# Five token blocks instead of six in two chained feed-forward networks, with rotating tiles for the halves of x

## The chip, the cores and the metric

The kernel runs on one core of a Trainium2 chip. The metric is the device time of one execution in microseconds (us). Before the change the median of three runs is 928.14 us (928.04 to 928.32).

## The reference

A window attention over 4 batches, 8 heads, 512 local and 32 global positions and head size 64 makes 2176 tokens of width 512. They pass through two feed-forward networks, one after the other, each with its own weights (512 x 2048 and 2048 x 512, given as float64):

```python
x = attention(q_l, k_l, v_l, q_g, k_g, v_g)   # 2176 x 512
h = x @ w_in;  x = (h * cos(h)) @ w_out       # network 0
h = x @ w2_in; out = (max(h, 0) ** 2) @ w2_out  # network 1
```

## The kernel before, in words

Every matrix is held as a high half and a low half in a reduced float32 format, and a product is three matmuls: high by high, low by high, high by low. The attention fills `xt`, the tokens by columns: 4 chunks (`kk`) of 128 features, 2176 columns. Then come the networks, which are one list of steps (`steps`). A step takes one block of token columns and one of the 16 chunks of 128 hidden units of its network (`g` 0 to 15 and 16 to 31). The chunks come in groups, 4, 5 and 7 in network 0 and 8 and 8 in network 1. Within a group the loop runs over the blocks, and within a block over the chunks of the group. So chunks 9 to 15 are first used in the first block of network 0's third group. With six blocks there are 96 steps in each network.

`ffn_step(s)` writes one step's instructions in a fixed order. On TensorE (PE) they are `g1` of step s (12 matmuls into `h`, one for each `kk` and each of the three products, as wide as the block), then `g2` of step s-3 into `y`. In network 0 `g2` is 12 matmuls as wide as the block; in network 1 the roles are turned, and it is three matmuls of width 512 for every 128 tokens of the block. ScalarE (ACT), VectorE (DVE) and GpSimd (POOL) do the rest, several steps interleaved, each engine strictly in the written order: ACT `ck` (L884), DVE L886, ACT cosine (L895), DVE product (L899), ACT high half `ghi` (L904), POOL low half `glo` (L910). In network 1 a ReLU on ACT (L890) stands in place of the first three. After a block's last `g2`, `y_evac` adds `y` to the partial sums (L857); in the last group of network 1 it writes `osb`, of which there are two buffers, and stores it.

`split_x` makes the halves of x for the next block, one `kk` at a time: ACT writes the high half (L801), DVE the low half (L802). Before, there are two sets of two tiles, each with all four `kk`, so the next block's set is free while the current one is read.

The weights come through `Feed`. A job is half a chunk (its part of `w_in` or of `w_out`). It is loaded by SyncE's queue (`raw`, two buffers), then in one stage for each call `conv_a` on ACT (L163, L164: `cu`, `cc`, two buffers each), `conv_b` on DVE (L172, L173) and `conv_c` on POOL (L183, into `r`). When both jobs of a chunk are done, `split` makes its halves `w`: two high ones on ACT (L246), then a low one each on POOL and DVE (L232). Each step earns 0.4 of a load (`RATE`). `g1` first calls `need`: if the chunk's `w` isn't written yet, jobs are run at one load a call until it is, and all their instructions stand on every engine ahead of the step's own:

```python
while g not in wtile:
    for op in self.begin(1.0):
        op()
    self.end()
    self.split(used)
```

Of the kernel before, what the change touches and what calls it, by code (L numbers as in the profile page):

```python
# [11 lines left out]
F32R = mybir.dt.float32r  # L12
# [7 lines left out]
P = 128  # L20
# [64 lines left out]
def kernel(  # L85
# [17 lines left out]
    NT, DM = out.shape  # L103
    DFF = w1_out.shape[0]
    NK = DM // P
# [2 lines left out]
    NR = NRING  # L108
    NLOC = B * SL
    NPAIR = H // 2  # L110
    BMAX = 384
    NA = 3

    ctx.enter_context(tc.manual_schedule())

# [3 lines left out]
    pools = {}  # L119
# [65 lines left out]
    class Feed:  # L185
# [40 lines left out]
        def split(self, used):  # L226
# [10 lines left out]
            if g >= 2 * NC or self.done < 2 * g + 2 or (g >= NSLOT and g - NSLOT not in used):  # L237
                return
            pool = pools.get("w0" if g % NSLOT < NA else "w1" if g % NSLOT < 5 else "w2")
            if pool is None:  # L240
# [14 lines left out]
    def bank(use, name):  # L255

        k = turn.get(use, 0)
        turn[use] = (k + 1) % len(use)
        return ps.tile([P, 512], F32, tag=f"bank{use[k]}", name=name)
# [445 lines left out]
    for h in range(2):  # L705
        s = slice(64 * h, 64 * h + 64)
# [34 lines left out]
    def weave(*lists):  # L741

        for group in zip_longest(*lists):
            for op in group:
                if op:
                    op()

    def it(k):
        return items[k] if 0 <= k < NI else None
# [6 lines left out]


    blocks = (
        [(364 * i, 364) for i in range(5)] + [(1820, NT - 1820)],
        [(384 * i, 384) for i in range(5)] + [(1920, NT - 1920)],  # L760
    )
    groups = GROUPS
    steps = []
# [12 lines left out]
    xsplit, hps, ctmp, gt, ghi = {}, {}, {}, {}, {}  # L776
    yps = []

    def block_start(s):

        while not steps[s][5]:
            s -= 1
        return s

    def left_in_block(s):
        k = s
        while k < NS and not steps[k][6]:
            k += 1
        return k - s + 1

    def split_x(s, kk):
        c0, n = steps[s][3]
        if kk == 0:
            k = len(xsplit) % 2
            xsplit[s] = [
                pools[f"x{k}"].tile([P, NK, BMAX], F32R, tag=f"x{k}{i}", name="x")
                for i in range(2)
            ]
        hi, lo = (t[:, kk, 0:n] for t in xsplit[s])
        xr = xt[:, kk, c0 : c0 + n]  # L800
        nc.scalar.activation(hi, xr, AF.Copy)  # L801
        return lambda: (nc.vector if kk in XD else nc.gpsimd).tensor_tensor(  # L802
            lo, xr, hi.bitcast(F32), op=ALU.subtract
        )

    def g1(s):
        net, _, _, (c0, n), g, _, _ = steps[s]
        feed.need(g, wused)
        w = wtile[g]
        hi, lo = xsplit[block_start(s)]  # L810
        h = bank(BH, "h")[:, 0:n]
        k = 0
        for kk in range(NK):
            for ws, x in ((0, hi), (1, hi), (0, lo)):
                nc.tensor.matmul(  # L815
                    h,
                    lhsT=w[:, ws, 0, kk * P : (kk + 1) * P],
                    rhs=x[:, kk, 0:n],
                    start=(k == 0),
                    stop=(k == 3 * NK - 1),  # L820
                )
                k += 1
        hps[s] = h

    def g2(s):
        net, _, _, (c0, n), g, c_first, c_last = steps[s]
        w = wtile[g]
        hi, lo = gt.pop(s)
        ne = NK if net == 0 else n // P
        if c_first:  # L830
            yps[:] = [bank(BY, "y") for e in range(ne)]
        for e in range(ne):
            sl = slice(e * P, (e + 1) * P)
            for k, (ws, x) in enumerate(((0, hi), (1, hi), (0, lo))):
                if net == 0:
                    o, l, r = yps[e][:, 0:n], w[:, ws, 1, sl], x
                else:
                    o, l, r = yps[e], x[:, sl], w[:, ws, 1, :]
                nc.tensor.matmul(  # L839
                    o, lhsT=l, rhs=r, start=(c_first and k == 0), stop=(c_last and k == 2)  # L840
                )
        if last_use[g] == s:
            wused[g] = s

    def y_evac(s):
        net, first, last, (c0, n), _, _, _ = steps[s]
        for e, y in enumerate(yps):
            if net == 0:
                y = y[:, 0:n]
                part, dst = ypart[0][:, e, c0 : c0 + n], xt[:, e, c0 : c0 + n]  # L850
            else:
                part = ypart[1][:, c0 // P + e, :]
                dst = pools["o"].tile([P, DM], F32, tag="osb", name="osb", bufs=2) if last else None
            if not last:
                dst = part
            if not first:
                nc.vector.tensor_tensor(dst, y, part, op=ALU.add)  # L857
            elif e % 2:
                nc.scalar.activation(dst, y, AF.Copy)
            else:  # L860
                nc.vector.tensor_copy(dst, y)
            if net == 1 and last:
                store(c0 // P + e, dst)
# [13 lines left out]
    def act_a(s):  # L877
        n = steps[s][3][1]
        r = pools["g"].tile([P, BMAX], F32, tag="cr", name="cr", bufs=4)[:, 0:n]
        ctmp[s] = r  # L880
        if steps[s][0] == 0:
            k = pools["g"].tile([P, BMAX], I32, tag="ck", name="ck", bufs=1)[:, 0:n]
            h = hps[s]
            nc.scalar.activation(k, h, AF.Copy, bias=0.25, scale=INV2PI)  # L884
            return [
                lambda: nc.vector.scalar_tensor_tensor(  # L886
                    r, h, INV2PI, k, op0=ALU.mult, op1=ALU.subtract
                ),
            ]
        nc.scalar.activation(r, hps[s], AF.Relu)  # L890
        return []

    def act_sin(s):
        if steps[s][0] == 0:
            nc.scalar.activation(ctmp[s], ctmp[s], AF.Sin, bias=halfpi, scale=TWOPI)  # L895

    def act_g(s):
        r = ctmp[s]
        nc.vector.tensor_tensor(r, hps.pop(s), r, op=ALU.mult)  # L899

    def act_hi(s):
        n = steps[s][3][1]
        ghi[s] = pools["g"].tile([P, BMAX], F32R, tag="ghi", name="ghi", bufs=LAG)[:, 0:n]
        nc.scalar.activation(ghi[s], ctmp[s], AF.Copy)  # L904

    def act_lo(s):
        n = steps[s][3][1]
        lo = pools["g"].tile([P, BMAX], F32R, tag="glo", name="glo", bufs=LAG)[:, 0:n]
        hi = ghi.pop(s)
        nc.gpsimd.tensor_tensor(lo, ctmp.pop(s), hi.bitcast(F32), op=ALU.subtract)  # L910
        gt[s] = (hi, lo)

    xq, xlo, yend = [], [], []
# [3 lines left out]
    def ffn_step(s):  # L917
        live = lambda k: 0 <= k < NS
        if yend:
            y_evac(yend.pop())  # L920
        if live(s):
            g1(s)
        if live(s - LAG):
            g2(s - LAG)
            if steps[s - LAG][6]:
                yend.append(s - LAG)
        if live(s - 2):
            act_hi(s - 2)
            act_lo(s - 2)
        if live(s - 1):  # L930
            act_sin(s - 1)
        lo, xlo[:] = xlo[:], []
        if live(s):
            if steps[s][5]:
                nxt = next((k for k in range(s + 1, NS) if steps[k][5]), None)
                xq[:] = [] if nxt is None else [(nxt, kk) for kk in range(NK)]
            for _ in range(2 if len(xq) > left_in_block(s) - 1 else 1):
                if xq:
                    xlo.append(split_x(*xq.pop(0)))
        cb = feed.begin(RATE)  # L940
        va = act_a(s) if live(s) else []
        for op in lo:
            op()
        if live(s - 1):
            va = [None, lambda: act_g(s - 1)] + va
        weave(cb, va)
        feed.end()
        feed.split(wused)
# [5 lines left out]
    for s in range(L["TRK"], NI + L["OE"]):  # L954
        due = lambda k: due_tr.get(s - k)
        cb, qe = [], []
        for c in CFG["order"]:
# [33 lines left out]
            else:  # L991
                i = it(s - L[c])
# [34 lines left out]
        if s in CFG["sx"]:  # L1027
            split_x(0, CFG["sx"].index(s))()
# [3 lines left out]
        if s >= NI:  # L1032
            ffn_step(s - NI)
# [5 lines left out]
    for s in range(L["OE"], NS + LAG + 1):  # L1039
        ffn_step(s)  # L1040
# [35 lines left out]
```

## Time and profile before

| what | value |
|---|---|
| median of three runs | 928.14 us |
| the profiled execution | 927.84 us |
| its span, first to last instruction or landing | 925.8 us |
| PE busy | 907.3 us (98%) |
| DVE, ACT, POOL busy | 516.3, 502.0, 427.7 us |
| mean granted clock of PE over the span | 0.999 |
| chain that ended last | 95% PE, of it `y` L839 41% and `h` L815 41% of the span |

The matmuls are pipelined: the busy time of one reaches into the next. How long one holds PE is read from the distance between the starts of two rows of the timeline, divided by the matmuls between them.

### The profile page before, as it was taken

How to read it: one execution, taken by the hardware profiler on the slowest of the kernel's cores; microseconds unless marked ns; L12 is line 12 of the kernel's file. 1: busy time of each engine (PE TensorE's matmuls, PEld its weight loads, DVE VectorE, ACT ScalarE, POOL GpSimd, SP SyncE). 2: the span in 40 equal slices, each digit the busy share in tenths (PEclk: the TensorE clock that was granted, in tenths of full speed). 3: DMA queues.
4: the chain of work that ended last, by engine and by line, in shares of the span. 5: the costliest groups of instructions: out<-in, count | busy, mean ns of one | idle time of the engine just before them, and what ended most of it. 6: DMA issues, size and time to landing. Idle time of an engine off the chain costs nothing.

```text
span 925.8 us, 16211 instructions
## 1 busy us (share of the span) xinstructions
PE 907.3 (98%) x5920; PEld 852.2 (92%) x5920; DVE 516.3 (56%) x1138; ACT 502.0 (54%) x1221; POOL 427.7 (46%) x523
## 2 busy tenths in 40 slices
PE   5999999999999999999999999999999999999997
PEld 4798888999999999999999999998989999999986
DVE  5777887766576665865555594443433932322312
ACT  3989998866665656655555573443223832222221
POOL 4777877544454433643334484333321942222221
PEclk9999999999999999999999999999999999999999
DMA  7667663212121112121112022111100100000001
GB/s 142 169 158 172 164 149 101 70 46 69 46 69 46 46 47 69 46 64 52 46 46 69 23 69 69 46 46 46 46 0 1 47 0 35 35 1 35 35 1 58
DMA packets 85071, 57.41 MB, mean 62 GB/s; under 512 B 60288, under 2 KB 76672, under 8 KB 84992
## 3 DMA queue, kind: packets, MB, share of 16 engines
q1 hardware_dynamic: 82848, 55.86, 21.5%
q8 instruction: 47, 0.77, 0.3%
q10 hardware_dynamic: 2144, 0.52, 0.3%
q14 instruction: 32, 0.26, 0.1%
HBM read 47.71 MB, written 4.46 MB: 56 GB/s over the span
## 4 chain that ended last, share of the span: by engine, by line
PE 95%; DMA 2%; DVE 1%; ACT 1%; POOL 1%; issue 0%; SPq 0%; POOLq 0%; DVEq 0%
PE y L839 41%; PE h L815 41%; PE s L454 3%; PE o L563 2%; PE tw L535 2%; PE tg L537 1%; PE og L672 1%; PE sg L593 1%; PE tq L397 1%; DMA kn<-in_k_l_dram 1%; PE o L551 1%; PE tk L360 1%; DMA qn<-in_q_l_dram 1%; DMA ktn<-in_k_l_dram 0%; POOL pt L501 0%; DVE pt L469 0%
## 5 line engine op out<-in xcount | busy, mean ns | idle before, releaser
L815 PE MATMUL h<-x,w 128*128 128x364 f32 (+3 forms) x2304 | 413.4, 328 | 0.0
L910 POOL TENSOR_TENSOR glo<-cr,ghi 128x364 fp32r<-128x364 f32 (+3 forms) x192 | 193.8, 1010 | 446.2 <-ACT ghi L904 388.4
L815 PEld LDWEIGHTS h<-x,w 128*128 128x128 f32 x2304 | 388.3, 188 | 8.1
L899 DVE TENSOR_TENSOR cr<-h,cr 128x364 f32<-128x364 f32 (+3 forms) x192 | 101.5, 529 | 196.3 <-ACT cr L890 167.7
L839 PE MATMUL y<-ghi,w 128*128 128x364 f32 (+1 forms) x768 | 189.4, 328 | 0.0
L839 PE MATMUL y<-w,ghi 128*128 128x512 f32 x544 | 169.4, 392 | 0.0
L890 ACT ACTIVATE cr<-h 128x384 f32<-128x384 f32 (+1 forms) x96 | 45.4, 473 | 223.0 <-PE h L815 222.9
L839 PEld LDWEIGHTS y<-ghi,w 128*128 128x128 f32 x768 | 135.9, 188 | 0.0
L839 PE MATMUL y<-glo,w 128*128 128x364 f32 (+1 forms) x384 | 126.0, 328 | 0.0
L839 PEld LDWEIGHTS y<-w,ghi 128*128 128x128 f32 x544 | 100.0, 188 | 16.3
L802 DVE TENSOR_TENSOR x<-xt,x 128x364 fp32r<-128x364 f32 (+3 forms) x120 | 109.1, 913 | 8.1 <-ACT x L801 8.1
L886 DVE SCALAR_TENSOR_TENSOR cr<-h,ck 128x364 f32<-128x364 f32 (+1 forms) x96 | 51.2, 534 | 109.6 <-ACT ck L884 106.6
L839 PE MATMUL y<-w,glo 128*128 128x512 f32 x272 | 107.4, 395 | 0.0
L904 ACT ACTIVATE ghi<-cr 128x364 fp32r<-128x364 f32 (+3 forms) x192 | 95.9, 500 | 20.1 <-DVE cr L899 19.7
L884 ACT ACTIVATE ck<-h 128x364 int32<-128x364 f32 (+1 forms) x96 | 45.1, 470 | 103.3 <-PE h L815 102.5
L183 POOL TENSOR_TENSOR r<-cu,cc 128x512 uint32<-128x512 uint32 x64 | 90.0, 1406 | 3.1 <-DVE cc L173 3.1
L839 PEld LDWEIGHTS y<-glo,w 128*128 128x128 f32 x384 | 72.3, 188 | 0.0
L895 ACT ACTIVATE cr<-cr,halfpi 128x364 f32<-128x364 f32 (+1 forms) x96 | 57.2, 596 | 17.2 <-DVE cr L886 17.2
L839 PEld LDWEIGHTS y<-w,glo 128*128 128x128 f32 x272 | 51.0, 188 | 11.0
L801 ACT ACTIVATE x<-xt 128x364 fp32r<-128x364 f32 (+3 forms) x120 | 58.6, 493 | 0.0
L479 ACT ACTIVATE pt<-pt,st 128x160 f32<-128x160 f32 x128 | 53.1, 419 | 3.2 <-DVE st L469 3.0
L173 DVE SCALAR_TENSOR_TENSOR cc<-raw,cc 128x512 uint32<-128x512 uint32 x64 | 52.1, 814 | 0.1
(97 smaller groups left out, 957.2 us busy)
## 6 DMA issues: line engine op xcount, KB each, us to landing
raw<-in_moe_w_in_dram SPq DMA_DIRECT2D x32, 512.0 KB, 3.6
raw<-in_moe_w_out_dram SPq DMA_DIRECT2D x32, 512.0 KB, 3.5
vb<-va SPq DMA_DIRECT2D x32, 128.0 KB, 2.5
out_dram<-osb SPq DMA_DIRECT2D x16, 256.0 KB, 2.0
qn<-in_q_l_dram SPq DMA_DIRECT2D x30, 128.0 KB, 2.8
kn<-in_k_l_dram SPq DMA_DIRECT2D x32, 96.0 KB, 3.5
va<-in_v_l_dram SPq DMA_DIRECT2D x32, 96.0 KB, 2.5
kn<-in_k_l_dram SPq DMA_DIRECT2D x16, 48.0 KB, 3.3
```

The costliest lines, as they stand in the source:

```text
L173: lambda: v.scalar_tensor_tensor(c, t[:, :, 1].bitcast(U32), 0x80000000, c, op0=ALU.bitwise_and, op1=ALU.bitwise_or,),
L183: nc.gpsimd.tensor_tensor(ring[g][:, q, :].bitcast(U32), u, c, op=ALU.add)
L479: nc.scalar.activation(self.pt[:, u, :], self.pt[:, u, :], AF.Exp, bias=self.st[:, 0, u : u + 1], scale=-1.0, accum_out=self.st[:, 1, u : ...
L801: nc.scalar.activation(hi, xr, AF.Copy)
L802: return lambda: (nc.vector if kk in XD else nc.gpsimd).tensor_tensor(lo, xr, hi.bitcast(F32), op=ALU.subtract)
L815: nc.tensor.matmul(h, lhsT=w[:, ws, 0, kk * P : (kk + 1) * P], rhs=x[:, kk, 0:n], start=(k == 0), stop=(k == 3 * NK - 1),)
L839: nc.tensor.matmul(o, lhsT=l, rhs=r, start=(c_first and k == 0), stop=(c_last and k == 2))
L886: lambda: nc.vector.scalar_tensor_tensor(r, h, INV2PI, k, op0=ALU.mult, op1=ALU.subtract),
L895: nc.scalar.activation(ctmp[s], ctmp[s], AF.Sin, bias=halfpi, scale=TWOPI)
L899: nc.vector.tensor_tensor(r, hps.pop(s), r, op=ALU.mult)
L904: nc.scalar.activation(ghi[s], ctmp[s], AF.Copy)
L910: nc.gpsimd.tensor_tensor(lo, ctmp.pop(s), hi.bitcast(F32), op=ALU.subtract)
```

## The change

Network 0's blocks become five of 436 (the last 432) instead of five of 364 and one of 356. Network 1's become two of 512 and three of 384 instead of five of 384 and one of 256. Each network has 80 steps instead of 96. `BMAX`, the width of the tiles, goes from 384 to 512.

The halves of x now lie in six pairs of tiles (`NX`), one `kk` each, used in turn. Two pairs are free while a block runs. So `kk` 0 and 1 of the next block are split in the first two steps of a block, and `kk` 2 and 3 in its last step, into tiles that this step's `g1` still reads.

```diff
-    BMAX = 384
+    BMAX = 512
     NA = 3
+    NX = 6
...
-        [(364 * i, 364) for i in range(5)] + [(1820, NT - 1820)],
-        [(384 * i, 384) for i in range(5)] + [(1920, NT - 1920)],
+        [(436 * i, 436) for i in range(4)] + [(1744, NT - 1744)],
+        [(0, 512), (512, 512)] + [(1024 + 384 * i, 384) for i in range(3)],
...
-            k = len(xsplit) % 2
-            xsplit[s] = [
-                pools[f"x{k}"].tile([P, NK, BMAX], F32R, tag=f"x{k}{i}", name="x")
-                for i in range(2)
-            ]
-        hi, lo = (t[:, kk, 0:n] for t in xsplit[s])
+            xsplit[s] = []
+        k = (NK * (len(xsplit) - 1) + kk) % NX
+        hi, lo = (
+            pools["x0" if k < NK else "x1"].tile([P, BMAX], F32R, tag=f"x{k}{i}", name="x")[:, 0:n]
+            for i in range(2)
+        )
+        xsplit[s].append((hi, lo))
...
-        for kk in range(NK):
+        for kk, (hi, lo) in enumerate(xsplit[block_start(s)]):
...
-            for _ in range(2 if len(xq) > left_in_block(s) - 1 else 1):
-                if xq:
-                    xlo.append(split_x(*xq.pop(0)))
+
+            if steps[s][6]:
+                while xq:
+                    lo.append(split_x(*xq.pop(0)))
+            elif len(xq) > 2 * NK - NX:
+                xlo.append(split_x(*xq.pop(0)))
```

`RATE` is unchanged, so the weights' loads are spread over fewer steps. Chunks 14 and 15 are first used in steps 59 and 60 before, and in steps 50 and 51 now.

ACT's order there, before: it begins with `ck` of step 56. `w_5307` is chunk 15, whose first `h` is that of step 60.

```order
L884 ACTIVATE ck_5301<-h_5267 128x364
L246 ACTIVATE w_5307<-r_5219 128x512 x2
L904 ACTIVATE ghi_5343<-cr_5257 128x364
L895 ACTIVATE cr_5300<-cr_5300,halfpi_70 128x364
L801 ACTIVATE x_5207<-xt_71 128x364
L163 ACTIVATE cu_5349<-raw_5298 128x512
L164 ACTIVATE cc_5350<-raw_5298 128x512
L884 ACTIVATE ck_5354<-h_5314 128x364
L904 ACTIVATE ghi_5386<-cr_5300 128x364
L895 ACTIVATE cr_5353<-cr_5353,halfpi_70 128x364
L884 ACTIVATE ck_5394<-h_5361 128x364
L904 ACTIVATE ghi_5426<-cr_5353 128x364
```

And now, from `ck` of step 49 (`h_5031`) on. `cu_5078` and `cu_5088` are the two jobs of chunk 15, `w_5083` is chunk 14, `cu_5126` is the first job of chunk 16, and `h_5096` belongs to step 50.

```order
L885 ACTIVATE ck_5066<-h_5031 128x436
L164 ACTIVATE cu_5078<-raw_5072 128x512
L165 ACTIVATE cc_5079<-raw_5072 128x512
L247 ACTIVATE w_5083<-r_5070 128x512 x2
L164 ACTIVATE cu_5088<-raw_5076 128x512
L165 ACTIVATE cc_5089<-raw_5076 128x512
L905 ACTIVATE ghi_5121<-cr_5024 128x436
L896 ACTIVATE cr_5065<-cr_5065,halfpi_70 128x436
L164 ACTIVATE cu_5126<-raw_5086 128x512
L165 ACTIVATE cc_5127<-raw_5086 128x512
L885 ACTIVATE ck_5131<-h_5096 128x436
L247 ACTIVATE w_5144<-r_5137 128x512 x2
```

Before, chunk 15's high halves stand four steps ahead of their use and one or no job lies between two `ck`. Now three jobs and chunk 14's high halves stand between `ck` of step 49 and `ck` of step 50, two of the jobs ahead of `ghi_5121` of step 48, and chunk 15's high halves stand behind `ck` of step 50.

POOL's order there, before: `r_5219` is chunk 15 before its split, `w_5223` chunk 14's low half, `w_5307` chunk 15's.

```order
L183 TENSOR_TENSOR r_5219<-cu_5119,cc_5120 128x512
L232 TENSOR_TENSOR w_5174<-r_4787,w_5174 128x512
L910 TENSOR_TENSOR glo_5253<-cr_5164,ghi_5251 128x356
L232 TENSOR_TENSOR w_5223<-r_4999,w_5223 128x512
L910 TENSOR_TENSOR glo_5294<-cr_5214,ghi_5292 128x364
L183 TENSOR_TENSOR r_5219<-cu_5210,cc_5211 128x512
L910 TENSOR_TENSOR glo_5345<-cr_5257,ghi_5343 128x364
L232 TENSOR_TENSOR w_5307<-r_5219,w_5307 128x512
L910 TENSOR_TENSOR glo_5388<-cr_5300,ghi_5386 128x364
L910 TENSOR_TENSOR glo_5428<-cr_5353,ghi_5426 128x364
```

And now, where `r_5070` and `w_5083` are chunk 14, `r_5137` and `w_5144` chunk 15, and `r_5153` is the first half of chunk 16. `glo_5123` belongs to step 48.

```order
L911 TENSOR_TENSOR glo_5058<-cr_4976,ghi_5056 128x436
L184 TENSOR_TENSOR r_5070<-cu_4972,cc_4973 128x512
L184 TENSOR_TENSOR r_5070<-cu_5061,cc_5062 128x512
L233 TENSOR_TENSOR w_5083<-r_5070,w_5083 128x512
L911 TENSOR_TENSOR glo_5123<-cr_5024,ghi_5121 128x436
L184 TENSOR_TENSOR r_5137<-cu_5078,cc_5079 128x512
L184 TENSOR_TENSOR r_5137<-cu_5088,cc_5089 128x512
L184 TENSOR_TENSOR r_5153<-cu_5126,cc_5127 128x512
L233 TENSOR_TENSOR w_5144<-r_5137,w_5144 128x512
L911 TENSOR_TENSOR glo_5184<-cr_5065,ghi_5182 128x436
```

Before, a `glo` stands between every two pieces of weight work but one. Now the last job and the low half of chunk 14 stand in a row, and behind one `glo` three jobs and the low half of chunk 15. On PE, `g1` of step 50 and of step 51 read these low halves with their second matmul.

## Rows read from the trace of the kernel before

**Rows 1.** Page, part 1: busy us of each engine, share of span, instructions.

```profile
PE 907.3 (98%) x5920; PEld 852.2 (92%) x5920; DVE 516.3 (56%) x1138; ACT 502.0 (54%) x1221; POOL 427.7 (46%) x523
```

**Rows 2.** Waits of PE from 155 to 921 us: total us, times, longest.

```profile
PE og L672 <- ACT tws L661: 0.2, 1, 0.2
```

**Rows 3.** Timeline of PE, first network, blocks of 364: start us, us, instructions.

```profile
301.21 2.16 PE L815 MATMUL h<-x,w 128*128 128x364 f32 x12
...
305.21 2.16 PE L815 MATMUL h<-x,w 128*128 128x364 f32 x12
```

**Rows 4.** The same where the block is 356 wide.

```profile
524.02 2.08 PE L815 MATMUL h<-x,w 128*128 128x356 f32 x12
...
527.86 2.08 PE L815 MATMUL h<-x,w 128*128 128x356 f32 x12
```

**Rows 5.** The same in the second network, block 384 wide.

```profile
560.07 2.27 PE L815 MATMUL h<-x,w 128*128 128x384 f32 x12
...
562.18 0.63 PE L839 MATMUL y<-w,ghi 128*128 128x512 f32 x2
...
564.26 2.27 PE L815 MATMUL h<-x,w 128*128 128x384 f32 x12
```

**Rows 6.** The same at the program's end, block 256 wide, then only y.

```profile
908.49 1.60 PE L815 MATMUL h<-x,w 128*128 128x256 f32 x12
...
909.92 0.63 PE L839 MATMUL y<-w,ghi 128*128 128x512 f32 x2
...
916.95 0.62 PE L839 MATMUL y<-w,ghi 128*128 128x512 f32 x2
...
917.63 0.62 PE L839 MATMUL y<-w,ghi 128*128 128x512 f32 x2
```

**Rows 7.** Groups by line and shape: count, busy us, mean ns, idle before.

```profile
L884 ACT ACTIVATE ck<-h 128x364 int32<-128x364 f32 x80 | 37.6, 471 | 88.2 <-PE h L815 87.4 <-PE y L839 0.4
...
L886 DVE SCALAR_TENSOR_TENSOR cr<-h,ck 128x364 f32<-128x364 f32 x80 | 42.8, 535 | 92.7 <-ACT ck L884 89.8 <-POOL w L232 2.8
...
L904 ACT ACTIVATE ghi<-cr 128x364 fp32r<-128x364 f32 x80 | 40.1, 502 | 11.1 <-DVE cr L899 11.1
...
L910 POOL TENSOR_TENSOR glo<-cr,ghi 128x364 fp32r<-128x364 f32 x80 | 80.2, 1002 | 172.4 <-ACT ghi L904 139.5 <-PE y L839 17.0 <-issue 12.3
...
L163 ACT ACTIVATE cu<-raw 128x512 f32<-128x512 f32 x64 | 42.2, 660 | 0.5 <-DMA raw<-in_moe_w_out_dram 0.5
...
L172 DVE TENSOR_SCALAR cu<-cu 128x512 uint32<-128x512 uint32 x64 | 42.0, 656 | 3.0 <-ACT cu L163 2.9
...
L173 DVE SCALAR_TENSOR_TENSOR cc<-raw,cc 128x512 uint32<-128x512 uint32 x64 | 52.1, 814 | 0.1
...
L183 POOL TENSOR_TENSOR r<-cu,cc 128x512 uint32<-128x512 uint32 x64 | 90.0, 1406 | 3.1 <-DVE cc L173 3.1
...
L232 POOL TENSOR_TENSOR w<-r,w 128x512 fp32r<-128x512 f32 x32 | 46.4, 1449 | 0.0
...
L802 DVE TENSOR_TENSOR x<-xt,x 128x364 fp32r<-128x364 f32 x60 | 52.6, 883 | 3.6 <-ACT x L801 3.6
...
L895 ACT ACTIVATE cr<-cr,halfpi 128x364 f32<-128x364 f32 x80 | 47.8, 598 | 15.1 <-DVE cr L886 15.1
```

**Rows 8.** DMA issues: KB each, median us from issue to landing.

```profile
raw<-in_moe_w_out_dram SPq DMA_DIRECT2D x32, 512.0 KB, 3.5
```

**Rows 9.** Timeline of DVE, evacuation of a 384-wide block in the last group.

```profile
772.72 0.69 DVE L857 TENSOR_TENSOR osb<-y,ypart 128x512 f32<-128x512 f32 x1 [1.58 <-DMA out_dram<-osb]
```

**Rows 10.** Timeline of DVE and SP's queue at the end.

```profile
920.55 1.37 DVE L857 TENSOR_TENSOR osb<-y,ypart 128x512 f32<-128x512 f32 x2 [3.88 <-PE y L839]
...
921.94 1.76 SPq L873 DMA_DIRECT2D out_dram<-osb  x4
```

**Rows 11.** Stretches after PE's last matmul: PE busy, PEclk, DMA share, GB/s.

```profile
922.50:923.50 1.00, 0.00 (x0) 1.00 0.79 232
923.50:924.50 1.00, 0.00 (x0) 0.69 0.54 135
```

More of the change, by code (lines that the diff above doesn't have):

```diff
@@ L809, in g1 @@
         w = wtile[g]
-        hi, lo = xsplit[block_start(s)]
         h = bank(BH, "h")[:, 0:n]
         k = 0
-        for kk in range(NK):
+        for kk, (hi, lo) in enumerate(xsplit[block_start(s)]):
             for ws, x in ((0, hi), (1, hi), (0, lo)):
@@ L817, in g1 @@
                     lhsT=w[:, ws, 0, kk * P : (kk + 1) * P],
-                    rhs=x[:, kk, 0:n],
+                    rhs=x,
                     start=(k == 0),
```

## The prediction

> **What bounds the kernel now.** Read the page's busy times first: PE is busy for 98% of the span [rows 1], but its matmuls overlap, so that is no proof. PE's waits are the proof: from 155 us, where the networks begin, to its last matmul at 921 us it waited 0.2 us in all [rows 2]. So both networks last as long as their matmuls hold PE, and nothing else counts until it makes PE wait. The timeline says how long one matmul holds it. At width 364 a step of 24 takes 4.00 us, 166.7 ns each [rows 3]; at 356, 3.84 us, 160.0 ns [rows 4]. In the second network 12 `h` matmuls of 384 take 2.11 us, 175.8 ns each, and the 9 `y` matmuls of 512 behind them 2.08 us, 231.1 ns [rows 5]. At the end, 12 of 256 take 1.43 us, 119.2 ns; and where only `y` is left, 3 of 512 take 0.68 us, 226.7 ns [rows 6].
>
> In cycles at 2.4 GHz the undisturbed ones are 286 for 256 columns, 384 for 356, 400 for 364 and 544 for 512: width plus 30, 28, 36 and 32. Since 8 columns more (356 to 364) cost 16 cycles, I read this as width plus 32 in steps of 16. Where widths alternate (384 and 512) there are some cycles more.
>
> **The change part by part.** *Fewer, wider matmuls, network 0.* The columns stay, and 16 x 24 = 384 matmuls go. Before: 80 steps x 4.00 + 16 x 3.84 = 381.4 us. 436 was never run. It lies 4 above a multiple of 16, as 356 does, so I take 436 + 28 = 464 cycles; 432 + 32 is 464 too. That is 193.3 ns, 4.64 us a step, 80 steps, 371.2 us: **10.2 us less**. The other end is the straight line from 175.8 ns at 384 to 231.1 at 512, 198.3 ns at 436: 380.7 us, 0.7 us less. I take the first, since the rows at 356 and 364 are pure streams of one width, as this will be, and those of the line are not.
>
> *Network 1.* Before: 80 steps x 4.19 [rows 5] + 16 x (1.43 + 6 x 0.231) = 335.2 + 45.1 = 380.3 us. After: the 48 steps of 384 stay at 4.19, 201.1 us. The 32 steps of 512 have 24 matmuls of one width; at the 226.7 ns of the pure stream [rows 6] that is 5.44 us, 174.1 us in all. Sum 375.2: **5.1 us less**; at 231.1 ns it would be 3.4 us more, 1.7 us less. I take 226.7, again the pure stream.
>
> The Trainium skill ("TensorE: Matmul & The Clock Gate", section "Back-to-back issue gap") gives the isolated warm gap between matmuls as width / 2.4 + 2.5 ns. The rows here disagree: 512 columns are 213.3 ns at 2.4 GHz, and the stream stands at 226.7, 13.3 ns above [rows 6].
>
> *Weights that come too late.* The loads earn their turn by the step, and chunk 14's first use moves from step 59 to 50. There one job of chunk 14 isn't converted yet, so `need` writes jobs ahead of `g1`, for chunk 14 and again for chunk 15 at step 51. PE is in order, so `g2` of step 47 stands behind the waiting `g1` too: PE has nothing else. I follow the chain from the start of `g1` of step 49 (time 0), with the durations of the groups [rows 7], those of the act operations scaled by 436/364 = 1.2.
> - `h` is done at 12 x 0.193 + 0.16 = 2.5; `ck` 0.56; L886 0.64, with the handoff at 3.8. DVE now converts chunk 14's second job: 0.66 + 0.81, at 5.3. POOL joins it, 1.41, at 6.7, and makes the low half, 1.45, at 8.1. PE's second matmul of step 50 would have started at 4.64 + 0.19 = 4.8: it waits 3.3 us.
> - The buffer of that job is free at 5.3, and chunk 15's second job is loaded into it: 3.5 us to landing [rows 8], 8.8. ACT is in order and stands at its conversion: 2 x 0.66, at 10.1; only then `ghi` of step 48, 0.60, at 10.7. POOL: `glo` 1.20, at 11.9, then chunk 15's first job, 1.41, at 13.3. That frees the `cu` buffer for which ACT waits with chunk 16's first job: 1.32, at 14.6. Then `ck` of step 50, 0.56, and on DVE L886, 0.64, at 15.8; behind it the conversion of chunk 16's job, 1.47, at 17.3; POOL joins it, 1.41, at 18.7, and last makes chunk 15's low half, 1.45, at 20.2.
>
> PE's second matmul of step 51 would have started at 2 x 4.64 + 0.19 = 9.5. **10.7 us more** in both waits. The means of the groups hold contended cases; a tenth less or more of the chain is 9 to 12 us, and nothing in it excludes either.
>
> *The clock.* In the second wait PE runs one matmul between about 13 and 20 us of that count. After the program's last matmul (modelled end 921.2) the granted clock was still 1.00 until 923.5, and 0.69 on average in the microsecond behind that [rows 11]: it fell to its lower level, 1.2 GHz, with PE idle. So I expect it to fall here too. A fall in the first wait costs nothing: PE would be back at the second wait before 20. Behind the second, each step at 1.2 GHz costs 4.64 us more. When the clock comes back no row shows; from below the bound is nothing, from above I set one whole step. I take half a step, **2.3 us more**.
>
> The Trainium skill (the same page, section "Why this matters for your kernels") warns that pauses between bursts of matmuls bring the half clock back; the fall behind the last matmul agrees, and it speaks against this change.
>
> *The end.* The last block now has three tiles of 128 tokens, not two, and `osb` two buffers, so the third addition waits for the first store. In the middle of the last group that wait was 1.58 us [rows 9]. At the end nothing hides it: before, the additions end 0.73 us after PE (921.92) and four stores follow, and they keep their length [rows 10]. **1.5 us more**.
>
> *At no cost, with their cover.* `kk` 2 and 3 of the next x, split in a block's last step: in that step ACT has at worst two copies of `y`, `ghi`, the cosine and these two, about 0.6 each, 3.6 us; the low halves on DVE, 0.88 x 1.2 = 1.06 each [rows 7], are out by 5.7. PE reads the last of them as matmul 12 of the next `g1`, at 4.64 + 11 x 0.193 = 6.8. Cover 1.1 us; gone, each of 24 edges would wait. Wider act operations have a longer step in proportion. Network 1 with four `y` tiles in five banks at 512 is what network 0 did before without a wait [rows 2].
>
> *Sum against the profiled execution* (927.84: the span of 925.8 and 2.0 around it): 927.84 - 10.2 - 5.1 + 10.7 + 2.3 + 1.5 = 927.0. The median of the runs lies 0.3 above that execution: **927.3 us**, 0.1% below before.
>
> **The rivals.** *The waits come, the clock is cheap* (it stays up, or is back at once) and the chain is a tenth shorter: no 2.3, and 9.6 in place of 10.7. 923.9, faster. For it: PE does run a matmul in the wait. Against: the fall at the end.
>
> *436 lies on the line, not on the step*: network 0 gains 0.7 in place of 10.2. 936.8, slower. It decides from 194.7 ns on, where 927.3 becomes 930.0. For it: every matmul in network 1 near it has more than 32 cycles over its width. Against: the pure streams.
>
> *512 stays at 231.1*: 3.4 more, 930.7, just slower. For it: all 80 steps of 384 have it, of which one stands here [rows 5]. Against: the stream at the end.
>
> *The block edges wait*: if the low half of `kk` 3 comes after 6.8, say by 0.3 us at 24 edges, 7.2 more: 934.5. For it: DVE also adds or copies `y` there. Against: the 1.1 us of cover.
>
> *What a matmul holds PE beyond its columns does not go with their number*: then the networks keep their 381.4 and 380.3 us, nothing stands against the other terms, and it is 942.6. Against: the cycles over the width are there at every width [rows 3 to 6]. The Trainium skill's gap, named above, lies near this: it would leave 384 x 2.5 ns = 1.0 us to gain.
>
> **How the numbers follow.** Chances: the forecast 0.44, the cheap clock 0.25, the line 0.10, the 512 at 231.1 0.12, the edges 0.07, the last 0.02. 0.2% is 1.9 us, about what a measurement of this kernel can tell from no change: 926.3 to 930.0 is "same". Within the forecast, the waits of 9 to 12 and the clock's 0 to 4.6 spread it from 923.5 to 931: 0.08 faster, 0.31 same, 0.05 slower. The cheap clock gives 0.21 faster, 0.04 same. The line, the edges and the last are 0.02 same, 0.17 slower; the 512 is split evenly. Faster 0.29, same 0.43, slower 0.28. The range 922.5 to 932.0 holds the forecast, the cheap clock and the 512, and leaves out the line, the edges and the last.
>
> **What would show it.** Steps of 4.64 us in network 0 and of 5.44 us in the blocks of 512 show the two gains; 4.76 and 5.55 are the line and the alternating rate. Two waits of PE for POOL's `w`, about 3 and 7 us and nowhere else, show the late weights; the granted clock just behind them shows the third term; a wait of about 1.5 us for `osb` behind PE's last matmul shows the fourth. PE waits for DVE `x` at the edges would show the fourth rival. I am wrong if the waits are hidden, or if the width costs otherwise than in steps of 16 cycles.

## The result: slower by 0.65%, and the profile after

The changed kernel takes 934.85 us (median of six runs, 932.43 to 936.06), the kernel before 928.23 (six runs, 927.57 to 929.65): ratio of all runs 1.0065, interval 1.005 to 1.0079 (the two medians alone would give 1.0071). The forecast of 927.3 was wrong, and the time lies above its range. The profiled execution is the shortest of the six, 932.43 us with a span of 930.6. Against the one of before (span 925.8) 4.8 us are to be explained; the rest to the median is taken up with the last two experiments.

The page first, part 1, as in [rows 1]:

```profile
PE 900.6 (97%) x5344; PEld 813.9 (87%) x5344; DVE 503.3 (54%) x1059; ACT 490.9 (53%) x1120; POOL 422.1 (45%) x491
```

576 matmuls fewer (384 in network 0, 192 in network 1) took only 6.7 us of busy time away. Then PE's waits from 150 us on (line waited for: us in total, times, longest), which answer [rows 2]:

```profile
PE h L816 <- POOL w L233: 6.2, 2, 3.5
PE h L816 <- ACT w L247: 2.0, 1, 2.0
...
PE h L816 <- DVE x L804: 0.8, 1, 0.8
```

These stand in the networks: two waits for POOL's low half of `w`, one for ACT's high half, one for the low half of x. The timeline of PE, rows of `h` alone, shows where (start us, us, instructions, idle before them and what ended it):

```profile
171.82 2.46 PE L816 MATMUL h<-x,w 128*128 128x436 f32 x11
...
175.04 0.47 PE L816 MATMUL h<-x,w 128*128 128x436 f32 x1 [0.75 <-DVE x L804]
...
177.72 2.54 PE L816 MATMUL h<-x,w 128*128 128x436 f32 x12
...
182.47 2.54 PE L816 MATMUL h<-x,w 128*128 128x436 f32 x12
...
386.26 2.53 PE L816 MATMUL h<-x,w 128*128 128x436 f32 x12
...
391.12 0.46 PE L816 MATMUL h<-x,w 128*128 128x436 f32 x1
...
394.26 2.45 PE L816 MATMUL h<-x,w 128*128 128x436 f32 x11 [2.67 <-POOL w L233]
...
401.06 0.47 PE L816 MATMUL h<-x,w 128*128 128x436 f32 x1 [1.98 <-ACT w L247]
...
405.06 4.37 PE L816 MATMUL h<-x,w 128*128 128x436 f32 x11 [3.54 <-POOL w L233]
...
411.68 2.48 PE L816 MATMUL h<-x,w 128*128 128x436 f32 x12
...
416.32 2.48 PE L816 MATMUL h<-x,w 128*128 128x436 f32 x12
```

Read the distances. 177.72 to 182.47 is a step of 24 in 4.75 us, 197.9 ns a matmul; 411.68 to 416.32 is 4.64 us, 193.3 ns. The width is the same and PE waits in neither. At 391.12 (step 50) and 401.06 (step 51) one matmul runs and the next eleven wait. From 405.06 to 411.68 23 matmuls take 6.62 us where 4.45 was due at 193.3 ns. The stretches there (window, PE busy, granted clock, DMA share, GB/s) say why:

```profile
395.00:400.00 5.00, 4.08 (x21) 1.00 0.56 191
400.00:405.00 5.00, 0.47 (x1) 0.77 0.30 95
405.00:410.00 5.00, 4.93 (x15) 0.55 0.03 9
410.00:415.00 5.00, 5.00 (x28) 1.00 0.33 111
```

The clock fell to 1.2 GHz inside the second wait (402.7 us) and came back while PE worked (409.5). The end, DVE's rows:

```profile
923.14 1.37 DVE L858 TENSOR_TENSOR osb<-y,ypart 128x512 f32<-128x512 f32 x2 [5.70 <-PE y L840]
...
926.01 0.69 DVE L858 TENSOR_TENSOR osb<-y,ypart 128x512 f32<-128x512 f32 x1 [1.50 <-DMA out_dram<-osb]
```

And network 1, a step of 512 and one of 384:

```profile
562.86 2.88 PE L816 MATMUL h<-x,w 128*128 128x512 f32 x12
565.58 0.62 PE L840 MATMUL y<-w,ghi 128*128 128x512 f32 x2
...
651.12 2.27 PE L816 MATMUL h<-x,w 128*128 128x384 f32 x12
...
655.30 2.27 PE L816 MATMUL h<-x,w 128*128 128x384 f32 x12
```

At 512, 12 take 2.72 us, 226.7 ns; the step of 384 is 4.18 us.

The terms, each as the distance in the trace of after against the one of before:

| term | forecast, us | measured, us |
|---|---|---|
| network 0, matmuls alone | -10.2 | -5.0 |
| network 1 | -5.1 | -4.5 |
| late weights | +10.7 | +9.1 |
| half clock behind them | +2.3 | +2.2 |
| the end | +1.5 | +1.5 |
| first block edge | 0 | +1.2 |
| start of the networks (first `h` at 155.57, before 155.03) | 0 | +0.5 |
| sum | -0.8 | +5.0 (spans: +4.8) |

Network 0 is about 27 steps at 4.64, 37 at 4.75 and 16 of the last block at 4.72 us, 376.4 against 381.4. The late weights: 405.06 less 386.26 is 18.8 us; at two steps of 4.75 and 0.2 it would be 9.7.

### The profile page after: what moved, and what is told of

Same layout as the page of the kernel before. It is cut to its first block, busy times and chain, and to the rows that moved or that the text cites. A ratio compares the mean times of both kernels' runs of the same rounds, so it can differ in the third digit from the quotient of the medians.

```text
span 930.6 us, 14804 instructions
## 1 busy us (share of the span) xinstructions
PE 900.6 (97%) x5344; PEld 813.9 (87%) x5344; DVE 503.3 (54%) x1059; ACT 490.9 (53%) x1120; POOL 422.1 (45%) x491
## 4 chain that ended last, share of the span: by engine, by line
PE 91%; DVE 2%; ACT 2%; DMA 2%; POOL 1%; issue 1%; SPq 0%; DVEq 0%; POOLq 0%; ACTq 0%
PE h L816 39%; PE y L840 39%; PE s L455 3%; PE o L564 2%; PE tw L536 1%; PE tg L538 1%; PE og L673 1%; PE tq L398 1%; PE sg L594 1%; PE o L552 1%; PE tk L361 1%; POOL pt L502 0%; DVE pt L470 0%; DMA kn<-in_k_l_dram 0%; DVE qbd L409 0%
## 5 line engine op out<-in xcount | busy, mean ns | idle before, releaser
L816 PE MATMUL h<-x,w 128*128 128x436 f32 (+3 forms) x1920 | 406.0, 360 | 8.9 <-POOL w L233 6.2
L911 POOL TENSOR_TENSOR glo<-cr,ghi 128x436 fp32r<-128x436 f32 (+3 forms) x160 | 185.5, 1159 | 448.0 <-ACT ghi L905 378.3
L840 PE MATMUL y<-ghi,w 128*128 128x436 f32 (+1 forms) x640 | 177.5, 358 | 0.0
L900 DVE TENSOR_TENSOR cr<-h,cr 128x436 f32<-128x436 f32 (+3 forms) x160 | 96.6, 605 | 130.8 <-ACT cr L891 112.8
L804 DVE TENSOR_TENSOR x<-xt,x 128x436 fp32r<-128x436 f32 (+3 forms) x100 | 97.0, 980 | 101.9 <-ACT x L803 85.9
L840 PEld LDWEIGHTS y<-w,ghi 128*128 128x128 f32 x544 | 101.4, 188 | 18.8
L840 PE MATMUL y<-glo,w 128*128 128x436 f32 (+1 forms) x320 | 114.6, 358 | 0.0
L905 ACT ACTIVATE ghi<-cr 128x436 fp32r<-128x436 f32 (+3 forms) x160 | 89.7, 561 | 25.9 <-DVE cr L900 24.8
L887 DVE SCALAR_TENSOR_TENSOR cr<-h,ck 128x436 f32<-128x436 f32 (+1 forms) x80 | 48.6, 607 | 98.5 <-ACT ck L885 97.2
L803 ACT ACTIVATE x<-xt 128x436 fp32r<-128x436 f32 (+3 forms) x100 | 55.1, 559 | 20.1 <-PE h L816 19.8
L840 PEld LDWEIGHTS y<-w,glo 128*128 128x128 f32 x272 | 51.0, 188 | 10.8
L896 ACT ACTIVATE cr<-cr,halfpi 128x436 f32<-128x436 f32 (+1 forms) x80 | 52.4, 656 | 10.9 <-DVE cr L887 10.9
```

Source lines behind the costliest of these rows:

```text
L816: nc.tensor.matmul(h, lhsT=w[:, ws, 0, kk * P : (kk + 1) * P], rhs=x, start=(k == 0), stop=(k == 3 * NK - 1),)
L840: nc.tensor.matmul(o, lhsT=l, rhs=r, start=(c_first and k == 0), stop=(c_last and k == 2))
L887: lambda: nc.vector.scalar_tensor_tensor(r, h, INV2PI, k, op0=ALU.mult, op1=ALU.subtract),
```

## The experiments

The kernel before ran on the same chip as each batch: 929.41 us (13 runs, 927.58 to 930.39) beside the rate of 0.5, network 0 in multiples of 128, network 0 alone and the streams; 928.38 (19 runs, 926.83 to 929.78) beside the lowered rate, network 1 alone, the many columns and the second stream kernel; 928.72 (one run) beside the last two. Diffs are against the changed kernel where nothing else is said.

**Are the late weights the loss?** More loads for each step, so that no job is left when a chunk is first used:

```diff
- 'rate': 0.4,
+ 'rate': 0.5,
```

> The changed kernel with RATE 0.5 in place of 0.4, so that no chunk of weights is made by need. Theory (the late weights cost 9.1 us of waits and 2.2 us of half clock, as the trace of the changed kernel shows): PE has no wait for POOL w, the clock stays at 2.4 GHz, and the time falls by about 11 us from 932.4 to 935, to 921 to 924; if the third group then stays at 197.8 ns a matmul as the first two do, 3 us of that are lost again (924 to 925). Rival (the loads come earlier and ACT, DVE and POOL are as late elsewhere, so that the wait moves): other PE waits of several us, 928 or more.

922.1 us (921.18 to 923.0), ratio 0.9929 [0.9912, 0.9945]: 12.75 us less than the changed kernel's median (12.6 by the two ratios to the kernel before), and faster than before. No wait for `w` is left, and the clock is up throughout. So the waits and the clock are the loss, as forecast: 9.1 + 2.2, and 1.2 of the edge, which has no wait here either, are 12.5. (Between the two profiled executions it is 11.2; there the first group of chunks is 1.1 us shorter here besides, and the third 2.3 longer, by the spacing of which now.) PE's timeline shows one thing more:

```profile
218.29 2.48 PE L816 MATMUL h<-x,w 128*128 128x436 f32 x12
...
222.93 2.48 PE L816 MATMUL h<-x,w 128*128 128x436 f32 x12
...
227.57 2.51 PE L816 MATMUL h<-x,w 128*128 128x432 f32 x12
...
265.45 2.54 PE L816 MATMUL h<-x,w 128*128 128x436 f32 x12
...
270.20 2.53 PE L816 MATMUL h<-x,w 128*128 128x436 f32 x12
```

436 ran at 193.3 ns (4.64 us a step) until the first block of 432, and at 197.9 (4.75) behind it, with no wait between. It stayed there to the end of network 0.

**The same with late weights, without the change.** The kernel before, with its rate lowered so that the same two chunks are written by `need`:

```diff
- 'rate': 0.4,
+ 'rate': 0.34,
```

> The kernel before with RATE 0.34 in place of 0.4, nothing else: need then makes chunks 14 and 15 in steps 59 and 60, with the same jobs left as in the changed kernel. Theory (the late weights cost what they do whatever the width): two PE waits for POOL w and one for ACT w, 8 to 10 us in all, and the clock falls behind the second wait for about 2 us more: 938 to 941. Rival (the wide blocks themselves made the chain long): under 5 us of waits, below 934.

940.69 us (940.56 to 940.99), ratio 1.0128 [1.0113, 1.0143], 12.3 us more. PE's timeline:

```profile
391.59 3.64 PE L815 MATMUL h<-x,w 128*128 128x364 f32 x11 [2.65 <-POOL w L232]
...
398.45 0.43 PE L815 MATMUL h<-x,w 128*128 128x364 f32 x1 [1.23 <-ACT w L246]
...
402.57 3.71 PE L815 MATMUL h<-x,w 128*128 128x364 f32 x11 [3.69 <-POOL w L232]
...
409.28 2.16 PE L815 MATMUL h<-x,w 128*128 128x364 f32 x12
```

The same three waits at width 364, and half clock behind the first of them (391.7 to 395.1 us) and in and behind the last (401.9 to 408.8): 402.57 to 409.28 is 6.71 us, where 23 matmuls at 166.7 ns are 3.83. The price belongs to the late weights, not to the wider blocks.

**Other widths for network 0.** The rate of 0.5, and blocks whose widths are all multiples of 128:

```diff
- 'rate': 0.4,
+ 'rate': 0.5,
...
- [(436 * i, 436) for i in range(4)] + [(1744, NT - 1744)],
+ [(0, 512), (512, 512)] + [(1024 + 384 * i, 384) for i in range(3)],
```

> As e1_rate, and network 0 in blocks of 512, 512, 384, 384, 384 like network 1. Theory (436 is a width at which the stream of matmuls can settle at two spacings, 193.3 and 197.8 ns; 512 and 384 stand at width plus 32 cycles, 226.7 and 173.3 ns): network 0's steps take 5.44 and 4.16 us, 373.8 us in all against about 379 in e1_rate, so 4 to 6 us faster than e1_rate, 917 to 920. Rival (after the waits at the start of the networks every width is 2% slower): 384 at 177 and 512 at 231 ns in network 0, no faster than e1_rate.

920.92 us (919.33 to 921.12), ratio 0.9909 [0.9894, 0.9924], the fastest of all that ran, 8.5 us under the kernel before. The steps were as expected, but beside the rate of 0.5 alone the gain was 1.2 us, not 4 to 6. In part that is the clock, which stood at its lower level from 155.4 to 158.9 us, where attention ends and the networks begin, and one `y` that waited 0.5 us for DVE (its step took 6.30 us where the three before it took 4.87); the rest was not followed up. The timeline of its 512:

```profile
180.70 2.88 PE L816 MATMUL h<-x,w 128*128 128x512 f32 x12
...
186.14 2.88 PE L816 MATMUL h<-x,w 128*128 128x512 f32 x12
```

5.44 us a step, 226.7 ns, in the first network too.

**Network 1 alone.** Network 0's blocks as before, rate 0.4:

```diff
- [(436 * i, 436) for i in range(4)] + [(1744, NT - 1744)],
+ [(364 * i, 364) for i in range(5)] + [(1820, NT - 1820)],
```

> The change in network 1 alone: network 0 keeps its blocks of 364 and 356, network 1 has 512, 512 and three of 384, with the six rotating tiles of x. No chunk is made by need (RATE 0.4). Theory (network 1 does what was forecast: 32 steps of 5.44 us in place of wider ones, 4.9 us less, and 1.5 us more behind PE's last matmul for osb): about 3.4 us faster than before on the same chip, ratio 0.996. Rival (the wide blocks or the six tiles cost waits of their own): PE waits for x or y in network 1, no faster than before.

927.42 us (926.48 to 929.83), ratio 0.9991 [0.9981, 1.0001]: 1.0 less, not 3.4. Network 1 ran as expected. The waits of PE (columns as above) show where it went:

```profile
PE h L816 <- DVE x L804: 0.8, 1, 0.8
```

The first edge cost 1.7 us in its step, one step of `y` took 0.7 more, the end 1.5. So the wait at the first edge comes with the new order of the halves, not with the width; and since the rate of 0.5 has the same order and no such wait, it takes the weights' work of rate 0.4 as well.

**Network 0 alone, without that wait.** Seven pairs of tiles, network 1's blocks as before, rate 0.5:

```diff
- 'rate': 0.4,
+ 'rate': 0.5,
...
-    BMAX = 512
+    BMAX = 436
-    NX = 6
+    NX = 7
...
- [(0, 512), (512, 512)] + [(1024 + 384 * i, 384) for i in range(3)],
+ [(384 * i, 384) for i in range(5)] + [(1920, NT - 1920)],
```

> The changed blocks of 436 in network 0 alone: network 1 has the blocks of before, BMAX is 436, NX is 7 (three of four kk of the next x are split early), RATE 0.5. Theory (the wait inside h at the first block edge puts the stream of 436 from 193.3 to 197.8 ns): if the wait at that edge goes, network 0 runs at 193.3 ns, 4.64 us a step, 371 us, and the time is about 918. Rival (436 goes to 197.8 ns whatever happens at the edge, the start at 193.3 was the exception): 4.75 us a step, 379 us, about 925.

928.52 us (10 runs, 927.4 to 929.72), ratio 0.9992 [0.9983, 1.0001]. No wait for x at the edge, and yet 436 stood at 198.4 to 198.6 ns, the means of its three groups. My theory, that the wait at the edge brings the longer spacing, fell. Here network 0 gained 1 us in all: 24 x (64 x 198.5 + 16 x 196.6) ns = 380.4 against 381.4. That is the rival "436 lies on the line" as it stood in the prediction, 0.7.

**The spacing by itself.** A kernel of streams, executed once: 36 matmuls of one width, four streams for each width. In the first two streams the first matmul waits, for its weights and then for its moving tile; in the other two it is the fourteenth that waits.

> Leaves out the whole computation (the output is zeros): streams of 36 matmuls of one width with a new weight tile each, for nine widths from 356 to 512, four streams a width: the first matmul waits for its weights or for its moving tile, or the 14th does. Theory (what the 14th matmul waits for decides the spacing behind it): 364, 384, 448, 480, 512 the same in all four streams (width plus 28 to 36 cycles), 436 at 193.3 ns where weights were waited for and at 197.8 where the moving tile was. Rival (the spacing goes by the width alone, and another engine's traffic made it 197.8): 193.3 ns at 436 in all four.

Timeline of PE, the runs of one width without a wait:

```profile
81.66 6.24 PE L91 MATMUL h<-x,w 128*128 128x384 f32 x35
...
154.23 7.09 PE L91 MATMUL h<-x,w 128*128 128x436 f32 x35
...
251.79 8.12 PE L91 MATMUL h<-x,w 128*128 128x512 f32 x35
```

The last matmul of 436 takes 0.36 us by itself, so 7.09 less that is 34 distances, 198 ns. It stands there in all four streams, whatever was waited for; for 436 both theories fell. 416 is another matter: it stands at 188.4 ns behind the waits for weights and at 186.7 behind those for the moving tile, and in the last two streams it goes from one to the other at the fourteenth matmul. The steady distances, and the cycles at 2.4 GHz over the width:

| width | 356 | 364 | 384 | 416 | 432 | 436 | 448 | 480 | 512 |
|---|---|---|---|---|---|---|---|---|---|
| ns | 160.0 | 166.7 | 173.3 | 186.7 or 188.4 | 196.0 | 197.8 | 202.6 | 216.7 | 226.7 |
| cycles over | 28 | 36 | 32 | 32 or 36 | 38 | 39 | 38 | 40 | 32 |

There is no step of 16 here: 432, 436 and 448 all lie 38 or 39 cycles over their width, and 384 and 512 lie 32.

**What ran before it.** The same kind of kernel, executed once, with 16 matmuls of another width ahead of each stream (those of 32 columns are also of another type, plain float32, with 64 weight columns).

> Leaves out the whole computation (the output is zeros): streams of 36 matmuls of 416, 436 or 464 columns, each behind 16 matmuls of 32, 64, 128, 256, 364 or 512 columns; behind those of 436 come 12 of 432 and 12 of 436 again. Theory (436 has two spacings, and what runs just before decides: behind narrow matmuls, as behind the attention's, it settles at 193.3 ns, and a change of width ends that): 193.3 ns behind 32 to 128 columns, 198 behind 364 and 512, and 198 for the 436 behind 432. Rival (the fast spacing needs the rest of the kernel, not the width before): 198 ns in all streams.

436 stood at 193.3 ns behind 32 and behind 512 columns, and at 197.8 behind 64, 128, 256 and 364; 416 at 186.7 behind 512 and 188.3 behind the others; 464 at 208.8 or 210. The 436 behind 432 stood at 197 to 198 ns in five streams, as expected, and at 193.4 in the one behind 128 columns, which had stood at 197.8 ahead of the 432. So one width has two spacings, and it can change in either direction where another width stands between. "Narrow ones make it short" did not hold: 64 and 128 gave the long one (the stream behind 64 also began at half clock, 89.2 to 92.6 us). The width ahead alone does not decide: the changed kernel, traced three times, has either spacing at the same place behind the same matmuls (its first group at 197.8, 197.8 and 193.3 ns, the last two traces below). What does stays open.

**More columns in few steps.** Rate 0.5, network 0 as in the fastest version, network 1 in four blocks of 512 and one of 128:

```diff
- 'rate': 0.4,
+ 'rate': 0.5,
...
- [(436 * i, 436) for i in range(4)] + [(1744, NT - 1744)],
- [(0, 512), (512, 512)] + [(1024 + 384 * i, 384) for i in range(3)],
+ [(0, 512), (512, 512)] + [(1024 + 384 * i, 384) for i in range(3)],
+ [(512 * i, 512) for i in range(4)] + [(2048, NT - 2048)],
```

> A try at a faster one: network 0 in 512, 512 and three of 384 as in e2_wide0, network 1 in four of 512 and one of 128, RATE 0.5. Theory (a matmul holds PE for width plus 32 cycles in streams of one width, and the last block has one tile of 128 tokens, so no wait for osb at the end): 64 steps of 5.44 and 16 of 1.5 us, 372 us for network 1 in place of 375, and 1.5 us less behind PE; about 4.5 us faster than e2_wide0, 916. Rival (steps of 1.5 us are shorter than the way through ACT, DVE and POOL, or osb's stores hold DVE up in them): PE waits for glo in those steps, 3 us or more of it lost.

929.24 us (10 runs, 926.3 to 932.02), ratio 1.0005 [0.9991, 1.0019], 8.3 us more than with 512 and 384, and 13 more than forecast. The longest wait of PE:

```profile
PE h L816 <- DVE cr L900: 1.1, 1, 1.1
```

Two things cost most of it. The 12 `h` of 128 columns take 1.29 us, 107.3 ns each, where the forecast had 66.7 (160 cycles): 16 steps x 12 x 40.6 ns are 7.8 us. In the second stream kernel 64 and 128 columns both stood at 111.6 ns, so with so few columns their number no longer set the distance. And behind the first block of 128 columns PE waited 0.73 us for x and 1.05 for DVE's product, and the clock fell (731.7 to 735.1 us): the two steps there took 10.8 us, the third 3.41, so 4.0 are lost. The clock also fell at the start (154.8 to 158.2). Fewer matmuls are no gain when some become this narrow.

**The changed kernel again, twice.** For what lies between the first profiled execution and the median.

> The changed kernel itself, profiled once more. Its profiled execution took 932.43 us, four of its other runs 934.8 to 936.1. If a run lands near 935, theory (the second spacing of 436): network 0's third group, 411.7 to 509 us, stands at 197.8 ns a matmul in place of 193.3, some 23 steps by 0.107 us = 2.5 us longer, and the waits for the late weights are as in the first trace, 18.8 us from the start of g1 of step 49 to the second matmul of step 51. Rival (the clock): network 0's third group keeps 193.3 ns and the stretch at half clock behind the second wait, or another at 155 us where the networks start, is about 2.5 us dearer.

932.51 us. PE's timeline:

```profile
394.02 4.37 PE L816 MATMUL h<-x,w 128*128 128x436 f32 x11 [2.68 <-POOL w L233]
...
404.89 2.44 PE L816 MATMUL h<-x,w 128*128 128x436 f32 x11 [3.12 <-POOL w L233]
...
409.55 2.54 PE L816 MATMUL h<-x,w 128*128 128x436 f32 x12
...
414.29 2.53 PE L816 MATMUL h<-x,w 128*128 128x436 f32 x12
```

The clock fell in the first wait (granted from 393.2 to 400.0 us at half), and PE was back at the second wait at 401.41, before the weights came at 404.89: it cost nothing. Behind the second wait the 23 matmuls took 4.66 us. That is 2 us less than in the first trace. But the third group now stands at 4.74 us a step: from 409.55 to the block of 432 at 509.23 it took 99.7 us, in the first trace 411.68 to 509.12, 97.4. So 2 us won and 2.3 lost, and the time is the same.

> The same kernel a second time, for the same question. If it lands near 932.4, both theories expect the first trace over again: the third group at 193.3 ns, half clock only from 402.7 to 409.5 us. If it lands near 935, as the run beside it.

934.0 us. PE's timeline:

```profile
404.94 3.97 PE L816 MATMUL h<-x,w 128*128 128x436 f32 x11 [3.54 <-POOL w L233]
...
411.12 2.54 PE L816 MATMUL h<-x,w 128*128 128x436 f32 x12
...
415.87 2.54 PE L816 MATMUL h<-x,w 128*128 128x436 f32 x12
```

The third group again at 4.75, 99.7 us long; 1.6 us of half clock behind the second wait; and the clock fell also at 155.7 to 159.1 us, so that from the first `h` to 172.84 it is 17.8 us in place of 16.3. The first group was at 193.3 ns here, 1.3 us less. Theory and rival both hold a part: the runs differ by the third group's spacing (2.3 us), by where the clock falls around the waits (up to 2) and by its fall at the networks' start (1.6). The first trace with the long third group and the fall at the start would be 936.3, and the longest run is 936.06. Neither execution lies near 934.85, so that the median's own executions are made of these pieces is argued, not shown. Their mean granted clocks fit it: of the six, the runs of 932.5 and 934.81 us both have 0.996, so of the 2.3 us between them the clock can be no more than the rounding, under 1 us.

## Why the prediction was wrong, step by step

**The failed step is the width.** "That is 193.3 ns, 4.64 us a step, 80 steps": 436 ran at 193.3 ns in about 27 steps of the profiled execution and at 197.8 in most others, so that network 0 gave 5.0 us, not 10.2. In two of the three traces the third group stood at 197.8 as well, which takes another 2.3 from the gain. The prediction kept the straight line, 198.3 ns, as its other end, and gave it a chance of 0.10 since it came from alternating widths and the pure streams at 356 and 364 did not show it. They could not: the "steps of 16 cycles" were read from those two widths, and the streams by themselves show that from 432 to 480 columns a matmul costs more over its columns than at 384 or 512. By the rule, 432, 448 and 480 columns would stand at 193.3, 200.0 and 213.3 ns; they stand at 196.0, 202.6 and 216.7. So the rule is wrong around 436, and that 436 at times runs at just the forecast 193.3 is luck. (The 256 columns that the prediction lists among the undisturbed alternate with `y` of 512; in the second stream kernel 16 of them in a row stand at 119.3 or 120.0 ns, so that figure holds.) With 5.0 in place of 10.2 the sum is 932.2, and the profiled execution took 932.43. Near that, smaller errors nearly cancel: the late weights were put 1.6 too dear, network 1's gain 0.6 too large, and 1.2 and 0.5 were left out.

**Late weights: right in place and chain.** Two waits for POOL's low half, 2.67 and 3.54 us idle, and between them one of 1.98 for ACT's high half, which the prediction did not name. The chain is that of the prediction: POOL's low half ends 7.9 us behind the start of `g1` of step 49 and PE goes on at 8.0 (forecast 8.1); ACT stands 1.44 us at the conversion of the job just loaded, then 1.98 us for the `cu` buffer. The rows of ACT and POOL in the timeline:

```profile
392.49 1.71 POOL L233 TENSOR_TENSOR w<-r,w 128x512 fp32r<-128x512 f32 x1
...
394.64 0.66 ACT L164 ACTIVATE cu<-raw 128x512 f32<-128x512 f32 x1 [1.44 <-DMA raw<-in_moe_w_out_dram]
...
398.85 0.66 ACT L164 ACTIVATE cu<-raw 128x512 f32<-128x512 f32 x1 [1.98 <-POOL r L184]
...
403.75 1.26 POOL L233 TENSOR_TENSOR w<-r,w 128x512 fp32r<-128x512 f32 x1
```

It ended at 18.8, not 20.2: the job that ACT stands for lands at 8.4 and not 8.8, DVE converts chunk 16's job in 1.0 us in place of 1.47, and the last `w` takes 1.26 in place of 1.45; most of the rest is ACT's, whose conversions follow each other 0.56 us apart where 0.66 was counted. With the longer undisturbed step (4.75) the two waits cost 9.1: inside the 9 to 12 that the prediction set.

**The clock: the fall was right, the size luck.** 2.2 against 2.3, but half a step was only the middle between nothing and a whole one, and the same kernel paid nothing in the second trace and 1.6 in the third, the kernel before with late weights 2.9. That a fall in the first wait costs nothing, as the prediction said, the second trace shows. The "cheap clock" rival is what the second trace has, with its chain at 9.2, but its gain went into the spacing. The Trainium skill's warning ("TensorE: Matmul & The Clock Gate", section "Why this matters for your kernels") agrees with the granted clock of 0.55 from 405 to 410 us; a lone matmul inside the pause did not keep the clock up.

**The end and network 1: right.** The third addition waits 1.50 us for the first store. The blocks of 512 stand at 226.7 ns, as in the pure stream of [rows 6]; the rival of 231.1 didn't come. Its steps are a little off at the turn from one width to the next.

**The cover at the block edges was wrong at one edge.** The rival priced 24 edges at 0.3 us; 1.2 us came, at the first edge alone. The prediction counted ACT's work of a step and left out what the weights add: a chunk's `split` and a job. The timeline of ACT and DVE there:

```profile
169.51 0.63 ACT L247 ACTIVATE w<-r 128x512 fp32r<-128x512 f32 x1 [1.97 <-POOL r L184]
...
172.16 1.01 ACT L803 ACTIVATE x<-xt 128x436 fp32r<-128x436 f32 x2
172.75 2.23 DVE L804 TENSOR_TENSOR x<-xt,x 128x436 fp32r<-128x436 f32 x2 [3.24 <-ACT x L803]
```

ACT stood 1.97 us for POOL at the high half of a later chunk. In order behind it came a job's conversion, `ghi`, the cosine and then both high halves of x: at 172.16, when PE had begun the `g1` that reads them. DVE's two low halves end at 175.0, where PE's last matmul of that step starts.

**"What a matmul holds PE beyond its columns does not go with their number"** fell: with the weights in time, 576 matmuls fewer make 0.7 to 0.9%. For network 0 by itself it nearly holds at the long spacing: 384 matmuls fewer made 1 us with the seven pairs of tiles. So in the profiled execution the change gains 9.5 us by its widths, and what stayed as it was, the loads earned by the step, costs it 11.3.

## What to carry to other kernels

When a loop gets fewer and longer steps, everything that is paid by the step (here the weights' loads) has to be set anew: one number decided between 0.65% slower and 0.7% faster. Measure what a matmul holds the engine at the very width that is to be used; two near widths told a rule that the third broke. In-order engines need their cover counted with everything that stands in the queue, the rare work too.

## What the runs showed of the hardware that I had not expected

- One width has two spacings: 436 columns at 193.3 or 197.8 ns, 416 at 186.7 or 188.4. In the changed kernel with rate 0.5, and in the last execution of the changed kernel, the short one lasted until the first block of 432 and didn't come back; in the first trace it came back behind the half clock at 411.68 and ended with the next block of 432. It is worth 2.3 us in the third group. What decides between them is open.
- In streams of one width 432 to 480 columns cost 38 to 40 cycles over their width, 384 and 512 cost 32, 356 only 28; and 64 and 128 columns take the same 111.6 ns.
- The clock can fall at the start of the networks, where PE waits 0.9 and 0.5 us at the end of attention; it did in 4 of the 10 traces with networks, and cost 1.6 us in the one where it was worked out. The kernel before may do the same: of its 32 runs beside the first two batches, the 13 with a mean granted clock of 0.999 or 1.0 took 926.8 to 928.8 us, the 19 with 0.997 or 0.998 928.4 to 930.4. No trace of a run of the second kind was kept, so where its clock fell is not shown.
